# Row broadcasts and relayouts of an attention and MLP kernel by way of DRAM scratch

## Chip, cores, metric

One core of a Trainium2 chip. The time is device microseconds (us) of that core for one execution. The kernel is already tuned: before the change it takes 1255.33 us (median of 2 runs, 1255.06 to 1255.6). Engines in the profile: PE is TensorE's matrix multiply, PEld its weight load, DVE VectorE, ACT ScalarE, POOL GpSimd, SP SyncE, whose queue (SPq) issues every DMA that matters here. In the profile's lines `arena` is the kernel's buffer in SBUF (on-chip memory of 128 partitions), `psum` the banks that matmuls write, and sums, recips, rstd and heads are the new scratch buffers in DRAM.

## The reference, cut to what matters

```python
B, S, D, H = 1, 2048, 640, 32            # head size Dh = 20
xn = layernorm(x)
# A: attention
q, k, v = split(xn @ wqkv)               # 32 heads
p = softmax(q @ k.T * Dh**-0.5)          # 2048 x 2048 for each head
s = (p @ v) @ wo
# B: an MLP over columns and rows
h  = gelu(layernorm(xn) @ w1)
x1 = xn + shift4(h) @ w2                 # four column groups shifted by +1, -1, +2, -2 rows
g  = silu(x1 + gelu(layernorm(x1) @ w3) @ w4)
out = x + s * g
```

Softmax is the heavy part. ACT does most of the 134 million exponentials (860 instructions of 128x1024 in the profile), DVE the rest with integer arithmetic on the score's bits.

## The kernel before

The program is a list of tasks, each with an engine, an assumed duration, buffers read and written. A planner in the kernel's own source simulates the chip with these assumptions and so fixes the order of instructions on every engine. On the chip each engine runs its list in that order and stands still where the next instruction's input is not there: DVE stood still 203.0 us in all, 9.5 at most, before the 31 multiplies below, until a DMA had landed. What the planner assumes of DMA is these lines (nanoseconds; nbytes is what the author of the task passed in):

```python
SYNC_LAT = 130.0
self.dma_bw = 280.0
self.dma_lat0 = 1900.0
...
if t.is_dma and t.nbytes:
    xs = max(t.finish, dma_free)                    # transfers queue behind each other
    dma_free = xs + t.nbytes / self.dma_bw
    t.lat = dma_free + self.dma_lat0 - t.finish
...
si = min(range(len(ps)), key=lambda i: ps[i][0])    # PSUM bank: the one free first
```

Heads are taken in 8 quads of 4, each against 4 blocks of 512 query columns: 32 groups. After a group, four heads' results stand in one PSUM bank, 32 partitions apart, each with its row of sums at partition 32i+20. Dividing needs the reciprocals of that row on all partitions of the head:

```python
def normalise(...):                                  # cut
    T("dve", ..., tensor_copy(Ob, PV))                               # ob
    # z: four rows of sums, one partition each, to 32 partitions x 16
    T("sp", 240, [dma_start(ZT[32*i:32*i+32, ob, :], Ob[32*i+20:32*i+21, :]...) for i in range(4)], nbytes=16384)
    T("dve", ..., reciprocal(RZ, ZT))                                # rz
    # ra: back to one partition of each head
    T("sp", 240, [dma_start(RB[32*i:32*i+1, :]..., RZ[32*i:32*i+32, ob, :]) for i in range(4)], nbytes=8192)
    # rb: from that partition to 19 others
    T("sp", 240, [dma_start(RB[32*i+1:32*i+20, :], <RB[32*i] read 19 times>) for i in range(4)], nbytes=128*2048)
    T("dve", ..., tensor_tensor(On, Ob, RB, op=mult))                # on
    # od: four or five DMAs of 20 partitions at most into OTd
```

For the MLP's first layernorm, the row of 2048 values of 1/std has to be on every partition:

```python
T("sp", 60, dma_start(RR[0:1, :]..., T16[0:NT, :]), nbytes=8192, name="rr0")
T("sp", 60, dma_start(RR[1:128, :], <RR[0] read 127 times>), nbytes=1048576, name="rr1")
...
T("dve", ..., tensor_tensor(y2c, xnT, RR, op=mult))                  # y2
```

Here 60 is the assumed cost of one issue on SP's queue in nanoseconds, 240 that of four. Query and key weights come in eight DMAs of 20 columns per quad, into a buffer whose other columns are zero.

Of the kernel before, what the change touches and what calls it, by code (L numbers as in the profile page):

```python
# [90 lines left out]
class Task:  # L91
# [3 lines left out]
                 "acq", "rel", "stream", "sidx", "cls", "nbytes", "mode", "ndma", "tile")  # L95

    def __init__(self, tid, eng, dur, fn, reads, writes, due, name, lat, is_dma):
# [27 lines left out]
        self.tile = None  # L125


class Planner:
# [75 lines left out]
    def task(self, eng, dur, fn, reads=(), writes=(), due=None, name="", lat=0.0,  # L204
             is_dma=False, acq=None, rel=None, stream=None, after=(), cls=0, nbytes=0, mode=0, ndma=1, tile=None):
# [6 lines left out]
        t.tile = tile  # L212
        if is_dma and nbytes:
            t.lat = self.dma_lat0 + nbytes / self.dma_bw
# [55 lines left out]
    def schedule(self, verbose=False):  # L270
        tasks = self.tasks
        n = len(tasks)
# [43 lines left out]
        while done < n:  # L316
# [52 lines left out]
            if t.acq is not None:  # L369
                pname, handle = t.acq  # L370
                ps = pstate[pname]
                si = min(range(len(ps)), key=lambda i: ps[i][0])
                ft, rel_tid = ps[si]
                handle.slot = si
                held[id(handle)] = (pname, si)
                ps[si] = (INF, None)
                if rel_tid is not None:
                    t.preds.add(rel_tid)
                    tasks[rel_tid].succs.append((t.id, True))
# [272 lines left out]

def c_pool(n, kind="ts"):
    return 150 + (1.1 if kind == "ts" else 2.4) * n


class Gen:
# [71 lines left out]
    def build(self, plan_only=False):  # L729
        nc, pl = self.nc, self.pl  # L730
        with contextlib.ExitStack() as es:
# [3 lines left out]
            pl.init_arena(ARENA)  # L735
            self.W0 = 5
# [47 lines left out]
    def setup_consts(self):  # L784
# [22 lines left out]
        zw = self.zw = self.alloc("zw", [32], BF16)  # L807
        T("pool", 200, lambda e: e.memset(zw[:, :], 0.0), writes=[A("zw")], name="zw")
# [3 lines left out]
    def alloc_persistent(self):  # L812
# [9 lines left out]
        self.Wp = self.alloc("Wp", [2, KC, 128], BF16)  # L822
        T("dve", 700, lambda e: e.memset(self.Wp[:, :, :, :], 0.0), writes=[A("Wp", qk) for qk in range(2)], name="wp0")
# [13 lines left out]
        T("pool", 600, lambda e: e.memset(self.RB[:, :], 0.0), writes=[A("RB")], name="rb0")  # L837
# [15 lines left out]
    def load_inputs(self):  # L853
# [4 lines left out]
        for n0 in range(0, cfg.NT, 2):  # L858
            n1 = n0 + 2
            T("sp", 60, lambda e, n0=n0, n1=n1: e.dma_start(X[:, n0:n1, :], xv[:, n0:n1, :]),  # L860
# [135 lines left out]
    def prep_weights(self, q):  # L996
# [4 lines left out]
        for qk in (1, 0):  # L1001
            c0 = qk * D + q * cfg.QW
            T("sp", 240, lambda e, qk=qk, c0=c0: [e.dma_start(self.Wp[:, qk, :, 32 * i:32 * i + DH], src[:, :, c0 + DH * i:c0 + DH * i + DH])
                                                 for i in range(4)],
              writes=[A("Wp", qk)], is_dma=True, nbytes=128 * cfg.KC * 64 * 8, name=f"ld_wp{q}_{qk}", stream=f"wp{qk}", ndma=4)

    def prep(self, q):
# [6 lines left out]
        KC, NQC = cfg.KC, cfg.NQC  # L1014
        KT, QT, Wp, xnT = self.KT, self.QT, self.Wp, self.xnT
        for qk, dst, tag in ((1, KT, "KT"), (0, QT, "QT")):
            for c in range(NQC):
                c0 = 512 * c
                at = [A(tag, b, c)] + ([A("QTa", b, c)] if qk == 0 else [])
                h, wa = self.mm_tile(f"{tag}{q}_{c}", KC, 512, lambda k, j, qk=qk: Wp[:, qk, k, 32 * j:32 * j + 32],  # L1020
                                     lambda k, j, c0=c0: xnT[:, k, c0:c0 + 512],
                                     lambda k, qk=qk, c=c: [A("Wp", qk)] + [A("xnT", k, c)], at)
                if qk == 1:
                    T("dve", c_dve(512), lambda e, h=h, c0=c0: e.tensor_scalar(KT[:, b, c0:c0 + 512], self.wbank(h)[:, 0:512],  # L1024
                                                                               self.eaug[:, 0:1], None, op0=ALU.add),
                      reads=[wa, A("eaug")], writes=at, name=f"kev{q}_{c}", rel=h)
                elif q == 0:
                    T("act", c_act(512) + 100, lambda e, h=h, c0=c0: e.activation(QT[:, b, c0:c0 + 512], self.wbank(h)[:, 0:512], AF.Copy),
                      reads=[wa], writes=at, name=f"qev{q}_{c}", rel=h)
                else:  # L1030
                    T("dve", c_dve(512), lambda e, h=h, c0=c0: e.tensor_copy(QT[:, b, c0:c0 + 512], self.wbank(h)[:, 0:512]),
                      reads=[wa], writes=at, name=f"qev{q}_{c}", rel=h)
# [21 lines left out]
        T("sp", 240, lambda e: [e.dma_start(QT[20:128:32, b, 512 * c:512 * c + 512], SH[32 * c:32 * c + 4, :]) for c in range(NQC)],  # L1054
# [3 lines left out]
    def v_load(self, hf):  # L1058
# [5 lines left out]
        self.T("sp", 60, lambda e: e.dma_start(Wv[:, :, :], src[:, :, c0:c0 + D // 2]), writes=[self.A(f"Wv{hf}")], is_dma=True,  # L1064
# [30 lines left out]
    def attn_quad(self, quad):  # L1095
# [9 lines left out]
        for qc in range(NQC):  # L1105
# [3 lines left out]
            if col:  # L1109
                T("sp", 240, lambda e, qc=qc, gb=gb: [e.dma_start(self.QM[32 * i:32 * i + 32, gb, i, :],  # L1110
# [96 lines left out]
    def score_dve(self, b, qc, kt, a, quad):  # L1207
# [6 lines left out]
        for jj in range(2):  # L1214
# [3 lines left out]
              acq=("W", h), mode=1)  # L1218
# [16 lines left out]
    def normalise(self, quad, qc):  # L1235
# [28 lines left out]
        def fz(e):  # L1264
            out = []
            for i in range(4):
                z = Ob[32 * i + 20:32 * i + 21, :].rearrange("o (a b) -> o a b", b=16)
                out.append(e.dma_start(ZT[32 * i:32 * i + 32, ob, :], z))  # L1268
            return out
        T("sp", 240, fz, reads=[A("Ob")], writes=[A("ZT", ob)], is_dma=True, nbytes=16384, name=f"z{quad}_{qc}", stream="z", ndma=4)  # L1270
        T("dve", c_dve(16, "recip"), lambda e: e.reciprocal(RZ[:, ob, :], ZT[:, ob, :]),  # L1271
          reads=[A("ZT", ob)], writes=[A("RZ", ob)], name=f"rz{quad}_{qc}")
        def fb(e):
            out = []
            for i in range(4):
                out.append(e.dma_start(RB[32 * i:32 * i + 1, :].rearrange("o (a b) -> o a b", b=16), RZ[32 * i:32 * i + 32, ob, :]))  # L1276
            return out
        T("sp", 240, fb, reads=[A("RZ", ob)], writes=[A("RB")], is_dma=True, nbytes=8192, name=f"ra{quad}_{qc}", stream="ra", ndma=4)
        def fc(e):
            out = []  # L1280
            for i in range(4):
                r = RB[32 * i:32 * i + 1, :]
                src = bass.AP(r.tensor, r.offset, [list(r.ap[0]), [0, 19], [1, 512]])
                out.append(e.dma_start(RB[32 * i + 1:32 * i + 20, :], src))  # L1284
            return out
        T("sp", 240, fc, reads=[A("RB")], writes=[A("RB")], is_dma=True, nbytes=128 * 2048, name=f"rb{quad}_{qc}", stream="rb", ndma=4)
# [5 lines left out]
        moves, ats = [], []  # L1292
        for i in range(4):
            r0, at = DH * (4 * quad + i), 32 * i
            while r0 < DH * (4 * quad + i + 1):
                st, p0 = divmod(r0, 128)
                L = min(128 - p0, DH * (4 * quad + i + 1) - r0)
                moves.append((at, st, p0, L))
                ats.append(A("OTd", st, qc))
                r0, at = r0 + L, at + L  # L1300
        def fd(e):
            return [e.dma_start(self.OTd[p0:p0 + L, st, 512 * qc:512 * qc + 512], self.On[at:at + L, ob, :]) for (at, st, p0, L) in moves]
        T("sp", 60 * len(moves), fd, reads=[A("On", ob)], writes=sorted(set(ats)), is_dma=True, nbytes=80 * 1024, name=f"od{quad}_{qc}",
          stream="od", ndma=len(moves))

    def load_wo(self):
# [10 lines left out]
        T("sp", 60, lambda e: e.dma_start(Wo[:, :, :], self.aps["A_wo"].rearrange("(kc p) n -> p kc n", p=128)),  # L1317
# [3 lines left out]
        T("sp", 240, lambda e: [e.dma_start(Wo7[32 * i:32 * i + DH, :], self.aps["A_wo"][r0 + DH * i:r0 + DH * i + DH, :]) for i in range(4)],  # L1321
# [19 lines left out]
    def finish_qc(self, qc):  # L1341
# [8 lines left out]
        for nl in range(4):  # L1350
            n = 4 * qc + nl
            sl = n % 2
            T("sp", 60, lambda e, sl=sl, n=n: e.dma_start(XR[:, sl, :], xs[:, n, :]),
# [23 lines left out]
            T("sp", 60, lambda e, sl=sl, n=n: e.dma_start(outv[:, n, :], OS[:, sl, :]),  # L1377
# [15 lines left out]
    def b_alloc1(self):  # L1393
# [14 lines left out]
          reads=[A("tv", 1), A("mh2")], writes=[A("R2")], name="r2")  # L1408
        RR = self.RR = self.alloc("RR", [S], FP32)
# [160 lines left out]
```

## Time and profile before

The lines of the profile themselves are quoted in the prediction below.

| path (before) | assumed by the planner | measured | shortfall | DVE waits in all |
|---|---|---|---|---|
| reciprocal to multiply (ra, rb), 31 groups | 0.24+1.93+0.24+2.84+0.39 = 5.6 us | 12.3 us, median | 6.7 us x 31 = 208 us | 203.0 us |
| 1/std to first product (rr0, rr1), once | 0.06+1.93+0.06+5.65+0.39 = 8.1 us | 42.5 us | 34.4 us | 34.1 us |

The issue cost was assumed at 60 ns each and is about 590 to 690 (median of the lines of z, ra and rb).

### The profile page before, as it was taken

How to read it: one execution, taken by the hardware profiler on the slowest of the kernel's cores; microseconds unless marked ns; L12 is line 12 of the kernel's file. 1: busy time of each engine (PE TensorE's matmuls, PEld its weight loads, DVE VectorE, ACT ScalarE, POOL GpSimd, SP SyncE). 2: the span in 40 equal slices, each digit the busy share in tenths (PEclk: the TensorE clock that was granted, in tenths of full speed). 3: DMA queues.
4: the chain of work that ended last, by engine and by line, in shares of the span. 5: the costliest groups of instructions: out<-in, count | busy, mean ns of one | idle time of the engine just before them, and what ended most of it. 6: DMA issues, size and time to landing. Idle time of an engine off the chain costs nothing.

```text
span 1255.6 us, 35173 instructions
## 1 busy us (share of the span) xinstructions
PE 989.7 (79%) x15986; PEld 403.3 (32%) x15986; DVE 703.4 (56%) x1143; ACT 900.6 (72%) x937; POOL 30.4 (2%) x61
## 2 busy tenths in 40 slices
PE   4944887878787897789977896878879799767786
PEld 2411332323222334244322442323323243222343
DVE  7713766656565466465744474544566446556425
ACT  6752977868678775478866987776588787667684
POOL 6000000000000001000000000000000000000000
PEclk9986988889888888899988898898898889888897
DMA  6100110001002100210111010110101100100122
GB/s 170 18 23 18 15 16 14 13 14 16 14 14 87 18 13 12 51 34 12 18 45 42 13 14 24 37 43 10 21 17 37 44 14 11 42 13 12 36 66 75
DMA packets 109629, 37.87 MB, mean 30 GB/s; under 512 B 89685, under 2 KB 106997, under 8 KB 109353
## 3 DMA queue, kind: packets, MB, share of 16 engines
q1 hardware_dynamic: 109480, 35.62, 12.2%
q8 instruction: 125, 2.05, 0.7%
q14 instruction: 24, 0.20, 0.1%
HBM read 20.09 MB, written 2.62 MB: 18 GB/s over the span
## 4 chain that ended last, share of the span: by engine, by line
PE 37%; DMA 27%; SPq 14%; DVE 12%; ACT 8%; issue 2%; ACTq 0%; DVEq 0%
DMA arena<-arena 26%; PE psum L722 13%; PE psum L1193 12%; ACT arena L1200 7%; SPq L1284 5%; PE psum L1175 4%; PE psum L1164 4%; SPq L1276 4%; SPq L1268 3%; DVE arena L1225 2%; PE psum L1153 2%; DVE arena L1138 2%; DVE arena L1287 1%; DMA arena<-in_B_w_dram 1%; DVE arena L882 1%
## 5 line engine op out<-in xcount | busy, mean ns | idle before, releaser
L1200 ACT ACTIVATE arena<-psum 128x1024 bf16<-128x1024 f32 x860 | 817.2, 1035 | 327.9 <-PE psum L1193 209.5
L722 PE MATMUL psum<-arena 128*32 128x320 bf16 (+1 forms) x6224 | 399.1, 356 | 75.1 <-DMA arena<-in_B_w_dram 16.3
L1193 PE MATMUL psum<-arena 128*32 128x512 bf16 x5344 | 441.7, 410 | 11.6 <-ACT arena L1200 9.1
L722 PEld LDWEIGHTS psum<-arena 128*32 128x32 bf16 x6224 | 166.1, 101 | 247.8 <-issue 54.9
L1175 PE MATMUL psum<-arena 32*128 32x512 bf16 x712 | 137.9, 410 | 99.1 <-DVE arena L1225 53.8
L1138 DVE TENSOR_SCALAR arena<-arena 128x2048 uint16<-128x2048 uint16 x328 | 208.5, 687 | 7.4 <-PE psum L1153 5.9
L1193 PEld LDWEIGHTS psum<-arena 128*32 128x32 bf16 x5344 | 122.3, 101 | 178.7 <-ACT arena L1200 108.8
L1164 PE MATMUL psum<-arena 128*22 128x512 bf16 x1720 | 172.7, 404 | 1.2 <-ACT arena L1200 1.2
L1225 DVE TENSOR_SCALAR arena<-psum 128x1024 uint16<-128x1024 f32 x114 | 138.6, 1216 | 43.4 <-PE psum L1175 42.3
L1153 PE MATMUL psum<-arena 128*22 128x512 bf16 x1312 | 119.6, 402 | 37.1 <-DVE arena L1138 36.8
L1287 DVE TENSOR_TENSOR arena<-arena 128x512 bf16<-128x512 f32 x31 | 21.5, 692 | 203.0 <-DMA arena<-arena 203.0
L1175 PEld LDWEIGHTS psum<-arena 32*128 32x128 bf16 x712 | 31.1, 92 | 222.2 <-DVE arena L1225 70.1
L1228 DVE TENSOR_SCALAR arena<-psum 128x512 uint16<-128x512 f32 x100 | 63.9, 680 | 20.1 <-PE psum L1175 19.6
L1164 PEld LDWEIGHTS psum<-arena 128*22 128x22 bf16 x1720 | 45.3, 95 | 66.8 <-issue 35.1
L1153 PEld LDWEIGHTS psum<-arena 128*22 128x22 bf16 x1312 | 34.4, 96 | 82.2 <-DVE arena L1138 47.2
L1508 DVE CAST arena<-psum 128x512 bf16<-128x512 f32 x48 | 32.9, 687 | 44.5 <-PE psum L722 44.4
L1521 DVE TENSOR_TENSOR arena<-psum,arena 128x320 bf16<-128x320 f32 x32 | 15.2, 488 | 42.6 <-PE psum L722 42.6
L1024 DVE TENSOR_SCALAR arena<-psum,arena 128x512 bf16<-128x512 f32 x32 | 23.8, 746 | 13.2 <-PE psum L722 13.2
L1271 DVE RECIPROCAL arena<-arena 128x16 f32<-128x16 f32 x31 | 7.8, 251 | 41.5 <-DMA arena<-arena 41.5
L1442 DVE TENSOR_TENSOR arena<-arena 128x2570 bf16<-128x2570 bf16 (+1 forms) x4 | 11.3, 2833 | 34.1 <-DMA arena<-arena 34.1
L1372 DVE SCALAR_TENSOR_TENSOR arena<-psum,arena 128x320 bf16<-128x320 f32 x32 | 15.1, 486 | 26.7 <-PE psum L722 26.7
L1467 DVE TENSOR_TENSOR arena<-psum,arena 128x320 bf16<-128x320 f32 x32 | 15.6, 487 | 17.5 <-PE psum L722 17.3
(83 smaller groups left out, 351.2 us busy)
## 6 DMA issues: line engine op xcount, KB each, us to landing
arena<-in_B_w_dram SPq DMA_DIRECT2D x48, 160.0 KB, 2.7
arena<-arena SPq DMA_DIRECT2D x124, 38.0 KB
arena<-arena SPq DMA_DIRECT2D x124, 32.0 KB, 1.8
arena<-arena SPq DMA_DIRECT2D x248, 2.0 KB, 1.7
arena<-in_A_x_dram SPq DMA_DIRECT2D x8, 320.0 KB, 5.9
arena<-in_A_x_dram SPq DMA_DIRECT2D x16, 160.0 KB, 2.4
out_dram<-arena SPq DMA_DIRECT2D x16, 160.0 KB, 2.0
arena<-arena SPq DMA_DIRECT2D x96, 20.0 KB
```

What stands on the lines that cost most here:

```text
L722: ins = e.matmul(pb[32 * c:32 * c + 32, 0:N], lhsT(k, c), rhs(k, c), start=(k == 0), stop=(k == nk - 1), tile_position=(0, 32 * c))
L1138: lambda e, s=s, v=v: e.tensor_scalar(SS[:, s, :], U[:, :], 0.5, EXP_B[v], op0=ALU.mult, op1=ALU.add),
L1153: ins = e.matmul(pb[32 * i:32 * i + 22, 0:512], w, SS[:, s, at:at + 512].bitcast(BF16), start=False, stop=final, tile_position=(0, 32 * i))
L1164: ins = e.matmul(pb[32 * i:32 * i + 22, 0:512], VA[:, ql, kts[i // 2], i, :], PT[:, slots[i // 2], 512 * (i % 2):512 * (i % 2) + 512], sta ...
L1175: return e.matmul(out, self.KT[32 * i:32 * i + 32, b, 128 * kt:128 * kt + 128], self.QT[32 * i:32 * i + 32, b, 512 * qc:512 * qc + 512], s ...
L1193: ins = e.matmul(self.bank(2 * sb + jj)[32 * c:32 * c + 32, :], self.KT[:, b, 128 * kt + 32 * c:128 * kt + 32 * c + 32], self.QM[:, gb, 2 ...
L1200: lambda e: e.activation(self.PT[:, slot, :], self.psum[:, 1024 * sb:1024 * sb + 1024], AF.Exp, scale=cfg.scale),
L1225: return e.tensor_scalar(dst, self.psum[:, 512 * (self.W0 + lo):512 * (self.W0 + hi + 1)], a_exp, EXP_BIAS, op0=ALU.mult, op1=ALU.add)
L1228: ins = e.tensor_scalar(dst[:, 512 * k:512 * k + 512], self.bank(self.W0 + s)[:, :], a_exp, EXP_BIAS, op0=ALU.mult, op1=ALU.add)
L1268: out.append(e.dma_start(ZT[32 * i:32 * i + 32, ob, :], z))
L1276: out.append(e.dma_start(RB[32 * i:32 * i + 1, :].rearrange("o (a b) -> o a b", b=16), RZ[32 * i:32 * i + 32, ob, :]))
L1284: out.append(e.dma_start(RB[32 * i + 1:32 * i + 20, :], src))
```

## The change

Six things are changed together. (1) The row of 1/std goes to DRAM and comes back to all 128 partitions in one DMA. (2) The chain of a group does the same: sums to DRAM, back as 128x16, reciprocals to DRAM, back as 128x512, one issue each. (3) A group's result goes to DRAM and back for the change of layout. (4) A quad's weights are loaded as 92 dense columns; the columns that belong to a neighbouring head are zeroed by a mask in the PSUM evacuation. (5) The planner picks PSUM banks so that two tiles that DVE could evacuate together lie side by side. (6) The planner assumes 660 ns for each DMA issue on SP in place of 60. The intent is a shorter chain: few DMAs, over many engines (the old row of 1/std ran at a DMA share of 0.06, a sixteenth).

```diff
# cut to its core; every other T("sp", 60, ...) also becomes T("sp", C_SP, ...)
+C_SP = 660
# (5) planner
-                si = min(range(len(ps)), key=lambda i: ps[i][0])
+                idle = [i for i in range(len(ps)) if ps[i][0] <= st + 1e-9]
+                if idle:
+                    ...                 # beside its partner, else at the edge or the middle
+                else:
+                    si = min(range(len(ps)), key=lambda i: ps[i][0])
# (2) chain; z and r0 (one DMA each) and back
-        T("sp", 240, fz, ..., name=f"z{quad}_{qc}", ndma=4)
+        T("sp", C_SP, lambda e: e.dma_start(dz[ob], Ob[20:128:32, :]), ..., nbytes=8192, name=f"z0{quad}_{qc}")
+        T("sp", C_SP, lambda e: e.dma_start(ZT[:, ob, :], dz[ob].rearrange("i (a b) -> (i a) b", b=16)), ..., nbytes=8192, name=f"z1{quad}_{qc}")
...
-        T("sp", 240, fb, ..., name=f"ra{quad}_{qc}", ndma=4)
-        T("sp", 240, fc, ..., name=f"rb{quad}_{qc}", ndma=4)
+        T("sp", C_SP, lambda e: e.dma_start(dr[ob].rearrange("i (a b) -> (i a) b", b=16), RZ[:, ob, :]), ..., nbytes=8192, name=f"r0{quad}_{qc}")
+        T("sp", C_SP, lambda e: e.dma_start(RB[:, :], bass.AP(dr.tensor, dr[ob].offset, [[512, 4], [0, 32], [1, 512]])), ...,
+          nbytes=128 * 2048, name=f"r1{quad}_{qc}")
# (3) heads
+        T("sp", C_SP, lambda e: e.dma_start(do[ob], self.On[:, ob, :]), ..., name=f"o0{quad}_{qc}")
+        ...                             # o1: do -> OTd, 1 to 4 DMAs
# (1) row of 1/std
-        T("sp", 60, lambda e: e.dma_start(RR[0:1, :]..., T16[0:NT, :]), name="rr0")
-        T("sp", 60, lambda e: e.dma_start(RR[1:128, :], bass.AP(RR.tensor, RR.offset, [list(RR[0:1, :].ap[0]), [0, 127], [1, S]])), name="rr1")
+        T("sp", C_SP, lambda e: e.dma_start(dq.rearrange("(n p) -> n p", p=128), T16[0:NT, :]), name="rr0")
+        T("sp", C_SP, lambda e: e.dma_start(RR[:, :], bass.AP(dq.tensor, dq.offset, [[0, 128], [1, S]])), name="rr1")
# (4) weights and mask
-            T("sp", 240, ... [e.dma_start(self.Wp[:, qk, :, 32*i:32*i+DH], src[:, :, c0+DH*i:c0+DH*i+DH]) for i in range(4)], ndma=4)
+            T("sp", C_SP, ... e.dma_start(self.Wp[:, qk, :, :], src[:, :, c0:c0 + 92]))
...
-    e.tensor_scalar(KT[...], psum, self.eaug[:, 0:1], None, op0=ALU.add)
+    e.tensor_scalar(KT[...], psum, mask[:, 0:1], self.eaug[:, 0:1], op0=ALU.mult, op1=ALU.add)
```

## The prediction

> **What bounds the kernel now.** I read the page's busy shares first, then the waits, then the timeline of one group, then busy time by stretch. There are 32 groups of attention (8 quads of heads, 4 column blocks each); after each but the last the 128x512 result must be divided by row sums which are carried to all partitions by DMA.
>
> ```profile
> PE 989.7 (79%) x15986; PEld 403.3 (32%) x15986; DVE 703.4 (56%) x1143; ACT 900.6 (72%) x937; POOL 30.4 (2%) x61
> PE 37%; DMA 27%; SPq 14%; DVE 12%; ACT 8%; issue 2%; ACTq 0%; DVEq 0%
> DMA arena<-arena 26%; PE psum L722 13%; PE psum L1193 12%; ACT arena L1200 7%; SPq L1284 5%; PE psum L1175 4%; PE psum L1164 4%; SPq L1276 4%; SPq L1268 3%; DVE arena L1225 2%; PE psum L1153 2%; DVE arena L1138 2%; DVE arena L1287 1%; DMA arena<-in_B_w_dram 1%; DVE arena L882 1%
> ```
>
> No engine is full, and 41% of the chain of work that ended last is DMA and its queue (the second line; the third is 26% for copies within SBUF alone). Who waits is in the view of waits (waiter, line, releaser: us in total, times, longest):
>
> ```profile
> ACT arena L1200 <- PE psum L1193: 209.5, 103, 34.5
> DVE arena L1287 <- DMA arena<-arena: 203.0, 31, 9.5
> DVE arena L1271 <- DMA arena<-arena: 41.5, 25, 4.8
> DVE arena L1442 <- DMA arena<-arena: 34.1, 1, 34.1
> ```
>
> L1287 is the multiply by the reciprocals, once per group: DVE stands still 203.0 us for it. L1271 is the reciprocal, L1442 the first product with the row of 1/std. ACT's exp (L1200) is the one that suffers, through PE. How, the timelines of DVE, PE and DMA queue show (start, us, ..., idle before and releaser in brackets):
>
> ```profile
> 512.20 0.69 DVE L1287 TENSOR_TENSOR arena<-arena 128x512 bf16<-128x512 f32 x1 [8.61 <-DMA arena<-arena]
> 512.81 1.22 DVE L1225 TENSOR_SCALAR arena<-psum 128x1024 uint16<-128x1024 f32 x1
> 514.08 1.47 PE L722 MATMUL psum<-arena 128*32 128x512 bf16 x12 [8.64 <-DVE arena L1225]
> 545.17 2.42 SPq L1268 DMA_DIRECT2D arena<-arena  x4
> 550.13 2.44 SPq L1276 DMA_DIRECT2D arena<-arena  x4
> 553.74 3.46 SPq L1284 DMA_DIRECT2D arena<-arena  x4
> ```
>
> DVE runs in a fixed order, so while L1287 waits it drains no PSUM; three working banks fill, PE stops (8.64 us), ACT runs dry. The last three lines are another group's chain: sums out (from 545.17), reciprocals in (550.13), rows spread (553.74, done when L1287 starts at 561.82). Busy time by stretch (window, length, PE, PEld, DVE, ACT, POOL, PE clock, DMA share, GB/s):
>
> ```profile
> 80.00:110.00 30.00, 0.00 (x0) 0.00 (x0) 1.26 (x1) 0.00 (x0) 0.00 (x0) 0.55 0.06 25
> 505.50:512.20 6.70, 0.00 (x0) 0.00 (x0) 0.00 (x1) 1.50 (x2) 0.00 (x0) 0.81 0.17 47
> 514.00:520.80 6.80, 6.28 (x68) 2.23 (x72) 3.72 (x7) 2.56 (x3) 0.00 (x0) 0.57 0.28 63
> 233.00:257.00 24.00, 23.67 (x418) 9.66 (x410) 16.23 (x27) 23.83 (x26) 0.00 (x0) 1.00 0.04 10
> sum 652.80, PE 615.50 PEld 253.63 DVE 453.22 ACT 590.66 POOL 4.26; mean PE 21.22 PEld 8.75 DVE 15.63 ACT 20.37 POOL 0.15
> ```
>
> First: for 30 us all engines stand still for the row of 1/std, with a DMA share of 0.06, one engine of sixteen. Second and third: a stall, then PE busy but at clock 0.57. Fourth: between stalls PE and ACT are both full. Last: the sum of 29 stretches, each from 8 us after one stall to the start of the next; there PE is 94% and ACT 90% busy.
>
> [...]127 rows of 8 KB in 40.7 us at share 0.06. [...]1.04 MB / 40.7 us = 25.6 GB/s. [...]Here a 2 KB SBUF copy lands in 1.7 us and a 160 KB store to DRAM in 2.0, so DRAM looks little dearer. [...]eight L1193 matmuls take 1.07 us after a stall, 0.61 otherwise.
>
> **The change part by part.**
> (1) Row of 1/std. Now 127 rows from one partition, one engine, 40.7 us. New: 8 KB to DRAM, then 128 rows[...]; with the write before it (2.0 against 1.7) about 7 us for what took 42.5. ACT's gap of 34.5 us goes but for 0 to 3: minus 33.
> (2) Chain of one group. Now, median over the 31 groups, 12.3 us from end of reciprocal to start of multiply, and about 4 from the copy of PSUM to the reciprocal. The pieces: 4 issues 2.4 us, 1.75 from last issue to landing, again 2.4 and 1.75, then 4 issues 3.46 and 5.73 to landing[...]. New, one issue each: sums to DRAM 2.0, back 2.1, reciprocal 0.25, to DRAM 2.1, broadcast. [...]So 4.1 up to the reciprocal (no gain) and 6.5 after it: estimate 10.8 against 16.5, 5.8 saved.
> (3) What DVE has to do meanwhile. In the built order I multiplied the instructions between the three by their mean times in the profile: before, 3.7 us ahead of the reciprocal and 5.4 between it and the multiply, on average; after, 6.0 and 5.7, because the planner now counts 660 ns per issue and four trips. Against 4.1 and 6.5, and with DVE 69% busy at the undisturbed pace (5.7 of work lasts about 8), most waits should vanish. A few groups have only 1 to 3.5 us of work in the second gap (worst 1.0, 1.4, 1.9, 3.3). Estimated rest: 15 to 40 us of DVE wait in all instead of 244.
> (4) Small things. Weights: 2 issues of 92 columns per quad in place of 8 of 20, off the path. Masking rides on evacuations that exist: 28 copies of 686 ns become multiplies from PSUM (like L1228's kind, 680 for the same size), 4 on ACT get a scale. Bank choice: 100 evacuations of 680 ns become 4, and 114 of 1216 become 162: 48 x (1360 - 1216) = 7 us of DVE, not its bound. Head transposes by way of DRAM have no reader until the end. PE and ACT keep every instruction of theirs.
>
> The sum, two ways. (a) From ACT's timeline: its idle inside the 31 DVE waits plus the 5 us after each is 191 us, of which 9% (15 us) is the ordinary pace of those 5 us: 176. With 33: minus 209, giving 1046. (b) From pace: from 115 to 1230 us ACT has 827 us of work; at 0.905 busy that takes 914. PE has 912 busy, of which 174 at half clock; at full clock (0.61/1.07) about 837, at 0.943 it takes 888. The slower, 914, replaces 1115: minus 201; with 33, minus 234, giving 1021. The middle, 1034, plus about 8 for remaining waits: 1040.
>
> **The rivals.** First, the wait moves: four dependent trips through DRAM could take 2.5 to 3 us each rather than 2 (the smallest loads of weights took 2.5), making 6.5 into 8 after the reciprocal. [...]Against: DVE has 5.7 us of work there. It would leave 2 us a group, some 60 us of DVE wait[...]: about 1085. Second, PE becomes the bound and gives the gain back: it needs 913 us at full clock in the whole kernel[...]. Against: in dense stretches the clock is 1.00, and the halves follow idleness. With the clock at 0.94 throughout: about 1090. Third, the DVE waits are hidden anyway, and only the 1/std row pays: 1220. Against: ACT is idle through and after most of them. Fourth, the SP queue, in order, waits between dependent trips, and holds weight loads for the MLP behind it (PE now waits 16.3 us for those): plus 10 to 30.
>
> **Range and chances.** Predicted 1040 us. 1000 would need a pace better than between stalls today; 1095 holds the first or second rival. Faster by over 2%: 0.97; within 2%: 0.02 (it would need the stalls and the row both to persist); slower: 0.01.
>
> **What would show each step.** (1) right if DVE's wait before the y product is under 4 us and all engines run through 80 to 110 us. (2) right if the stretch from reciprocal to multiply, where DVE does wait, is 6 to 7 us, with the broadcast 4 to 4.5 from issue to landing. (3) right if the DVE wait at the multiply falls from 203 to under 40 and the PE clock's mean rises from 0.89 to above 0.95. The pace is right if ACT between 115 us and the end's last 25 is about 90% busy. I am wrong if the DVE waits go and ACT stays below 85% busy, which would mean another bound I did not see, or if the multiply still waits over 3 us a group.

The forecast came to 1040 us: sum (a) 1046, sum (b) 1021, their middle 1034, plus about 8 for remaining waits. Some terms of the sum: in (1) the copy to 128 rows, 4.6 us of the "about 7"; in (2) the new broadcast, 4.3 us of the 6.5 after the reciprocal. 4.6 and 4.3 were estimates; nothing had shown them then. "One engine" is read off a DMA share of 0.06, a sixteenth.

## The result, and the profile after

After: 975.93 us median (974.78 and 977.09) against 1255.33; ratio 0.7774, interval 0.7734 to 0.7814. A ratio here is the mean time of one kernel's fast runs over that of the other's in the same rounds, so not quite the ratio of the medians quoted. All runs were fast, except one of before (1264.88 us, in the rounds of e7, e10, e11 and e12), which the ratios leave out; all gave correct results. The prediction was 1040 with a range from 1000 to 1095: the direction was right, the time is 24 us under the range.

The page after: busy shares, then the chain of work that ended last by engine.

```profile
PE 905.6 (93%) x15986; PEld 382.8 (39%) x15986; DVE 706.0 (73%) x1096; ACT 888.6 (91%) x937; POOL 29.7 (3%) x59
PE 49%; ACT 39%; DVE 6%; DMA 4%; issue 1%; SPq 0%; POOL 0%; DVEq 0%
```

PE was at 79% and is at 93%, with the same 15986 instructions; its busy time fell by 84 us at a higher clock (0.888 and 0.993, below), and the mean of 5344 score matmuls (L1193, after L1213) from 410 to 381 ns. DMA and its queue held 41% of the chain that ended last and hold 4%. PE and ACT now share it, 49 and 39%. The row of granted PE clock over 40 slices (tenths), before and after:

```profile
PEclk9986988889888888899988898898898889888897
```

```profile
PEclk9999999999999999999999999999999999999998
```

The mean went from 0.888 to 0.993. A slice of before is 31 us, about one group long, and so held a stall and the low clock after it (0.57 in 514 to 520.8 us) nearly every time.

The waits of the kernel after (waiter, line, releaser: us in total, times, longest). L1295 is the multiply, L1289 the reciprocal, L1220 ACT's exp:

```profile
DVE arena L1295 <- DMA arena<-recips: 15.7, 14, 2.3
DVE arena L1289 <- DMA arena<-sums: 1.0, 2, 0.7
ACT arena L1220 <- PE psum L1184: 42.2, 21, 9.1
```

The multiply waited 203.0 us and waits 15.7; the reciprocal 41.5 and now 1.0. ACT's largest wait for PE was 209.5 us and is 42.2. No line is left in which DVE waits for the row of 1/std: the product with it ran at 63.40 us, straight behind other work, in the timeline. The same view has one group's chain (start, us, engine, line; idle before in brackets), near the same time as the one that the prediction shows:

```profile
63.40 2.83 DVE L1460 TENSOR_TENSOR arena<-arena 128x2570 bf16<-128x2570 bf16 x1
...
515.46 0.25 DVE L1289 RECIPROCAL arena<-arena 128x16 f32<-128x16 f32 x1
515.74 0.34 SPq L1291 DMA_DIRECT2D recips<-arena  x1
517.97 0.58 SPq L1293 DMA_DIRECT2D arena<-recips  x1
523.30 0.69 DVE L1295 TENSOR_TENSOR arena<-arena 128x512 bf16<-128x512 f32 x1 [1.97 <-DMA arena<-recips]
```

From the end of the reciprocal (515.71) to the multiply (523.30) are 7.6 us, and here DVE did wait, so this is the chain's own length: 2.2 to the second issue, then 0.58 of issue and 4.75 to landing. Over all groups the median is 7.8 us where it was 12.3. What single transfers take is in the list of DMAs (size of each, median us to landing):

```profile
arena<-rstd SPq DMA_DIRECT2D x1, 1024.0 KB, 4.7
arena<-sums SPq DMA_DIRECT2D x31, 8.0 KB, 1.7
recips<-arena SPq DMA_DIRECT2D x31, 8.0 KB, 1.4
```

The row of 1/std, 40.7 us before, lands in 4.7, and small trips to and from DRAM take 1.4 to 1.7 in the median.

Busy time by stretch (window, length, PE, PEld, DVE, ACT, POOL, PE clock, DMA share, GB/s). First the main stretch of before, then three of after, which together hold the same work and the tail:

```profile
115.00:1230.00 1115.00, 912.48 (x14510) 366.50 (x14506) 632.60 (x987) 826.68 (x839) 7.13 (x15) 0.89 0.11 26
```

```profile
78.00:115.00 37.00, 34.49 (x594) 13.33 (x590) 27.93 (x37) 36.94 (x39) 0.00 (x0) 1.00 0.09 25
115.00:945.00 830.00, 794.47 (x13876) 330.99 (x13868) 606.59 (x902) 781.64 (x806) 7.07 (x15) 1.00 0.16 42
945.00:973.00 28.00, 18.59 (x420) 10.35 (x420) 16.92 (x37) 12.76 (x14) 0.00 (x0) 0.88 0.27 84
```

The counts nearly match: 839 ACT instructions before, 844 after (39+806, one of them counted on both sides of 115). Work that began at 115 now begins at about 78, or at 82.9 if one goes by the same ACT instruction, the 87th; so the row of 1/std and what went with it gave back 32 to 37 us. From 78 to 945 are 867 us in place of 1115; ACT is busy 818.6 of them (36.94+781.64), 94.4%. That percentage is where the prediction went wrong.

### The profile page after: what moved, and what is told of

It is laid out like the page before. It is cut to its first block, busy times and chain, and to the rows that moved or that the text cites. A ratio compares the mean times of both kernels' runs of the same rounds, so it can differ in the third digit from the quotient of the medians.

```text
span 973.1 us, 34801 instructions
## 1 busy us (share of the span) xinstructions
PE 905.6 (93%) x15986; PEld 382.8 (39%) x15986; DVE 706.0 (73%) x1096; ACT 888.6 (91%) x937; POOL 29.7 (3%) x59
## 3 DMA queue, kind: packets, MB, share of 16 engines
q1 hardware_dynamic: 80132, 43.09, 15.9%
## 4 chain that ended last, share of the span: by engine, by line
PE 49%; ACT 39%; DVE 6%; DMA 4%; issue 1%; SPq 0%; POOL 0%; DVEq 0%
ACT arena L1220 36%; PE psum L738 19%; PE psum L1213 17%; PE psum L1184 5%; PE psum L1195 4%; PE psum L1173 3%; DMA arena<-recips 3%; DVE arena L1245 1%; ACT arena L1530 1%; DVE arena L1158 1%; DMA arena<-in_B_w_dram 1%; DVE arena L901 1%; ACT arena L1543 1%; DVE arena L1460 1%; DVE arena L1043 1%
## 5 line engine op out<-in xcount | busy, mean ns | idle before, releaser
L1220 ACT ACTIVATE arena<-psum 128x1024 bf16<-128x1024 f32 x860 | 805.1, 1039 | 56.9 <-PE psum L1184 42.2
L1213 PE MATMUL psum<-arena 128*32 128x512 bf16 x5344 | 408.2, 381 | 14.9 <-ACT arena L1220 12.3
L738 PE MATMUL psum<-arena 128*32 128x320 bf16 (+1 forms) x6224 | 366.2, 336 | 14.9 <-DVE arena L1043 6.5
L1245 DVE TENSOR_SCALAR arena<-psum 128x1024 uint16<-128x1024 f32 x162 | 197.5, 1219 | 62.0 <-PE psum L1195 60.8
L738 PEld LDWEIGHTS psum<-arena 128*32 128x32 bf16 x6224 | 161.2, 97 | 161.0 <-issue 23.5
L1213 PEld LDWEIGHTS psum<-arena 128*32 128x32 bf16 x5344 | 107.9, 95 | 172.3 <-ACT arena L1220 136.4
L1184 PE MATMUL psum<-arena 128*22 128x512 bf16 x1720 | 163.3, 381 | 0.1
L1195 PE MATMUL psum<-arena 32*128 32x512 bf16 x712 | 125.3, 385 | 11.8 <-ACT arena L1220 6.4
L1173 PE MATMUL psum<-arena 128*22 128x512 bf16 x1312 | 112.9, 380 | 1.9 <-DVE arena L1158 1.7
L1526 DVE CAST arena<-psum 128x512 bf16<-128x512 f32 x48 | 33.1, 689 | 42.6 <-PE psum L738 42.6
L1539 DVE TENSOR_TENSOR arena<-psum,arena 128x320 bf16<-128x320 f32 x32 | 15.7, 491 | 38.4 <-PE psum L738 38.2
L1295 DVE TENSOR_TENSOR arena<-arena 128x512 bf16<-128x512 f32 x31 | 21.3, 687 | 15.8 <-DMA arena<-recips 15.7
L1043 DVE TENSOR_SCALAR arena<-psum,arena 128x512 bf16<-128x512 f32 x32 | 25.5, 803 | 4.5 <-PE psum L738 4.4
L1474 DVE CAST arena<-psum 128x512 bf16<-128x512 f32 x20 | 13.8, 689 | 18.0 <-PE psum L738 18.0
L1282 DVE COPY arena<-psum 128x512 f32<-128x512 f32 x31 | 21.3, 688 | 6.2 <-PE psum L1184 5.9
L1050 DVE TENSOR_SCALAR arena<-psum,arena 128x512 bf16<-128x512 f32 x28 | 20.8, 747 | 5.9 <-PE psum L738 5.7
```

The costliest lines, as they stand in the source:

```text
L738: ins = e.matmul(pb[32 * c:32 * c + 32, 0:N], lhsT(k, c), rhs(k, c), start=(k == 0), stop=(k == nk - 1), tile_position=(0, 32 * c))
L1043: T("dve", c_dve(512), lambda e, h=h, c0=c0: e.tensor_scalar(KT[:, b, c0:c0 + 512], self.wbank(h)[:, 0:512], mask[:, 0:1], self.eaug[:, 0: ...
L1173: ins = e.matmul(pb[32 * i:32 * i + 22, 0:512], w, SS[:, s, at:at + 512].bitcast(BF16), start=False, stop=final, tile_position=(0, 32 * i))
L1184: ins = e.matmul(pb[32 * i:32 * i + 22, 0:512], VA[:, ql, kts[i // 2], i, :], PT[:, slots[i // 2], 512 * (i % 2):512 * (i % 2) + 512], sta ...
L1195: return e.matmul(out, self.KT[32 * i:32 * i + 32, b, 128 * kt:128 * kt + 128], self.QT[32 * i:32 * i + 32, b, 512 * qc:512 * qc + 512], s ...
L1213: ins = e.matmul(self.bank(2 * sb + jj)[32 * c:32 * c + 32, :], self.KT[:, b, 128 * kt + 32 * c:128 * kt + 32 * c + 32], self.QM[:, gb, 2 ...
```

## The experiments

Four questions were asked: which of the six parts pays; which of the planner's costs; whether the route by DRAM pays as such or only because the planner's assumption comes true with it; and what limits a row broadcast. My theory at first was that the DRAM route shortens the chain and so removes the waits. The rivals: the planner's issue cost (6) orders the work better, whatever the route; bank choice (5) saves DVE work; and, later, the planner's ignorance of DMA times is the whole trouble. Letters in the expectations are names for such theories. The kernels ran on four chips, on which before took 1250 to 1259 us in the median; the ratios allow for that, the medians do not. Where a difference is small both are given; a difference of 0.001 in the ratio is 1.3 us. The summary:

| run | built from | median us (range) | ratio to before, interval |
|---|---|---|---|
| after | | 975.93 (974.78-977.09) | 0.7774, 0.7734-0.7814 |
| e1_nobank | after, old bank choice | 976.41 (974.49-979.7) | 0.7756, 0.7718-0.7795 |
| e2_oldcost | after, issue cost 60 | 1003.69 (998.48-1008.02) | 0.7982, 0.7934-0.803 |
| e3_routes_only | after, both planner changes undone | 1008.67 (1004.91-1011.3) | 0.8008, 0.7968-0.8047 |
| e4_bank_only | before, new bank choice | 1256.52 (1252.79-1266.65) | 0.9991, 0.993-1.0052 |
| e10_chaincost | after, 660 for the chain only | 988.68 (987.01-992.5) | 0.7897, 0.7849-0.7945 |
| e11_othercost | after, 660 for all but the chain | 984.57 (982.65-984.92) | 0.7856, 0.7821-0.7891 |
| e12_longchain | after, 1300 for the chain | 974.52 (974.01-976.31) | 0.7781, 0.7746-0.7816 |
| e17_w3cost | e10 and MLP weight loads | 985.21 (983.0-991.19) | 0.784, 0.7786-0.7894 |
| e18_qmcost | e10 and query copies | 983.6 (982.13-987.2) | 0.7824, 0.7765-0.7883 |
| e6_bank_cost | before, (5) and (6) | 1047.77 (1046.58-1049.82) | 0.8373, 0.8336-0.8409 |
| e7_honest | e6, planner told true landings | 988.14 (986.24-989.49) | 0.7886, 0.785-0.7922 |
| e14_honest_rr | e7, 1/std by DRAM | 978.02 (977.84-979.86) | 0.7817, 0.7784-0.785 |
| e8_oldrr | after, old 1/std row | 1018.07 (1016.32-1022.93) | 0.814, 0.81-0.8179 |
| e9_sbrr | after, 1/std from one partition to 128 | 1010.76 (1008.27-1013.94) | 0.8084, 0.8041-0.8126 |
| e16_tree | after, 1/std within SBUF in two steps | 983.03 (982.25-984.35) | 0.7816, 0.7769-0.7863 |
| e20_spread | e16, middle rows four apart | 978.18 (975.75-979.84) | 0.777, 0.7714-0.7826 |
| e13_r1x4 | after, spread as four DMAs | 973.99 (972.55-976.29) | 0.7745, 0.7698-0.7792 |

### Which part pays

e1_nobank undoes the bank choice in the kernel after. It tells whether part (5) is worth the few us of DVE that the prediction gave it.

```diff
-                idle = [i for i in range(len(ps)) if ps[i][0] <= st + 1e-9]
-                ...
+                si = min(range(len(ps)), key=lambda i: ps[i][0])
```

> The changed kernel with the old choice of PSUM bank (lowest free time) put back, all else changed. Theory E (the pace between the old stalls was still slowed by them; the DMA routes alone bring the gain): 975 to 990 us, DVE waits at the multiply still under 30 us. Rival B (the pace came from pairs of score tiles in neighbouring banks, which spare DVE's split evacuations and PE's waits for banks): 1005 to 1030 us, with about 100 evacuations of 680 ns back and PE waiting over 40 us for them.

976.41, the same as after. The bank choice is worth nothing that can be measured here.

e2_oldcost undoes only the planner's issue cost.

```diff
-C_SP = 660
+C_SP = 60
```

> The changed kernel with the planner told 60 ns per DMA issue as before, all else changed. Theory E: 975 to 995 us; the planned chain becomes some 2.4 us shorter than real, so DVE waits at the multiply grow from 16 to 40-70 us but stay under 3 us each[...]. Rival C (the pace came from the planner's true issue cost, which orders all engines better): 1010 to 1040 us.

1003.69, 28 us slower than after (26 by the ratios), which lies between the two ranges. With 60 assumed, DVE waits 31.3 us at the multiply and 8.7 at the reciprocal, against 15.7 and 1.0. Nothing that moves data differs from the kernel after; only the order does. So a number in the planner is worth 28 us.

e3_routes_only undoes both (the two edits above), which leaves the routes by DRAM and the dense weights.

> The changed kernel with both planner changes undone: DMA routes, dense weights and mask alone. Theory E: 980 to 1005 us. B and C together: 1035 to 1060 us, near the forecast of 1040.

1008.67: parts (1) to (4) alone take 247 of the 279 us; this too lies between the two ranges, 4 us over the first. The intervals of e2 and e3 overlap, so the bank choice is not seen here either.

e4_bank_only puts the bank choice into the kernel before, in the same lines as the change has it.

> The kernel before with the new bank choice alone. Theory E: 1245 to 1256 us (7 us of DVE work less, stalls unchanged at 203 us). Rival B: 1215 to 1235 us.

0.9991: nothing. Theory E's upper end was 1256, the run took 1256.52.

### Which of the planner's costs

e10_chaincost assumes 660 ns for the four DMAs of the chain alone (z0, z1, r0, r1) and 60 for all others; e11_othercost the reverse. If the gain of part (6) came from DVE's wait at the multiply, e10 should have it in full.

```diff
-C_SP = 660
+C_SP = 60
+C_CH = 660
-        T("sp", C_SP, lambda e: e.dma_start(dz[ob], ...
+        T("sp", C_CH, lambda e: e.dma_start(dz[ob], ...      # also z1, r0, r1; e11: C_SP = 660, C_CH = 60
```

> The changed kernel, planner told 660 ns only for the four DMAs of the normalise chain and 60 ns for all other DMAs. Told 60 ns for all, it took 1004 us; told 660 for all, 976. Theory D (what the true cost buys is distance: DVE's multiply is placed later, and each us of DVE wait saved is a us of time): 976 to 985 us, DVE wait at the multiply 15 to 20 us. Rival S (it buys a better order of the in-order DMA queue and of all else): 995 to 1005 us.

> The complement: 60 ns for the chain's four DMAs, 660 ns for all others. Theory D: 995 to 1005 us, DVE wait at reciprocal and multiply about 40 us together. Rival S: 976 to 985 us.

988.68 and 984.57. Each half gives part of it; e10 is in neither range, e11 in that of rival S. e11, whose DVE waits at the multiply are 32.0 us, twice those of e10 (14.4), is if anything the faster (4 us in the same rounds, the runs' ranges apart). So DVE's wait is not what these us go by. One thing that the other issues do change is in the view of waits: PE's wait for the streamed MLP weights, before, after and in e10 (one line of each).

```profile
PE psum L722 <- DMA arena<-in_B_w_dram: 16.3, 8, 4.0
```

```profile
PE psum L738 <- DMA arena<-in_B_w_dram: 0.3, 1, 0.3
```

In e10 this wait is 6.2 us. That is a part of the 12.7 us between e10 and after at most.

e17_w3cost and e18_qmcost add one kind of issue to e10 each, to find the one that matters: the loads of MLP weights, or the copies of queries.

```diff
-T("sp", C_SP, lambda e, ws=ws, fc=fc: e.dma_start(W3s...          # e17; C_SP is 60
+T("sp", 660, lambda e, ws=ws, fc=fc: e.dma_start(W3s...
-T("sp", 4 * C_SP, lambda e, qc=qc, gb=gb: [e.dma_start(self.QM... # e18
+T("sp", 2640, lambda e, qc=qc, gb=gb: [e.dma_start(self.QM...
```

> Planner told 660 ns for the chain and for the 48 loads of MLP weights, 60 ns for the rest (with the chain alone it was 988.7, with all 976). Theory W (PE's 6 us of waits for these weights and what follows from them make the difference): 975 to 980 us, PE's wait for them under 1 us. Otherwise 985 to 990.

> Planner told 660 ns per issue for the chain and for the 124 query copies (2.6 us a group), 60 ns for the rest. If these make the difference: 975 to 980 us. Otherwise 985 to 990.

985.21 and 983.6: neither gives the 12.7 us alone (3.5 and 5 by the medians, 7 and 9 of 15 by the ratios), and their ranges overlap. PE's wait for weights is 4.0 and 1.8 us. Which issue costs improve the order, and how, stays open.

e12_longchain tells the planner that the chain is longer still (C_CH = 1300, others 660), so that it puts more work between reciprocal and multiply. If what is left of DVE's waits still costs time, this should gain; the theory that it does expected 958 to 968.

> The changed kernel, planner told 1300 ns for each of the chain's four DMAs, 660 for the others: 2.6 us more distance per group. Theory D: the 16.7 us of DVE waits fall under 4 us and the time to 958 to 968 us. Rival: DVE's multiply is no longer what limits, 973 to 980 us.

```profile
DVE arena L1296 <- DMA arena<-recips: 3.9, 5, 1.3
```

The multiply waits 3.9 us in all in place of 15.7, and the time is 974.52, the same. So the waits of after, 2.3 us at most, cost nothing that can be measured. The theory fell.

### The route, or the plan?

e6_bank_cost is the kernel before with the planner's two changes and none of the routes: every 60 becomes 660, every 240 becomes 2640.

```diff
-        T("sp", 240, fc, ..., name=f"rb{quad}_{qc}", ndma=4)
+        T("sp", 2640, fc, ..., name=f"rb{quad}_{qc}", ndma=4)     # and so for all; bank choice as in (5)
```

> The kernel before with both planner changes (bank choice, 660 ns per issue) and all its old DMAs and their assumed landing times. The twelve issues of a group's chain now count 7.2 us more. Theory P (the planner's ignorance was the cost): DVE waits at the multiply fall from 203 to 20-60 us, the gap of the 1/std row stays at some 30 us, time 1025 to 1060. Rival R (the routes by themselves): over 1150 us.

1047.77: 208 of the 279 us, with every DMA still the old one. Its waits:

```profile
DVE arena L1300 <- DMA arena<-arena: 50.6, 25, 4.4
DVE arena L1455 <- DMA arena<-arena: 35.2, 1, 35.2
```

The multiply's wait (L1300) fell from 203.0 to 50.6 us. The row of 1/std (L1455) keeps its wait in full, for its time was mistaken in the assumed bytes per ns and not in the issue.

e7_honest goes on from e6 and corrects these two as well. It passes the planner sizes that make the assumed landings true (3.57 + 1.9 = 5.5 us for rb, 38.2 + 1.9 = 40.1 for rr1). The DMAs themselves are still those of before. If the chain's length is what costs, this stays near e6; if it is the order, it comes near to after.

```diff
-  ... nbytes=128 * 2048, name=f"rb{quad}_{qc}"
+  ... nbytes=1000000, name=f"rb{quad}_{qc}"
-  ... nbytes=1048576, name="rr1"
+  ... nbytes=10700000, name="rr1"
```

> The kernel before with its old one-partition DMAs, but new bank choice, 660 ns per issue, and the planner told the landing times measured (about 5.5 us for the spread, 40 us for the row of 1/std). Theory P (what cost the time was that the planner did not know the DMAs were slow; slow but known they can be hidden): 985 to 1030 us, DVE wait at the multiply under 60 us. Rival R (the slow routes cost by themselves[...]): 1080 to 1200 us.

988.14, which is 267 of the 279 us and faster than the routes alone (e3). One group in its timeline (L1284 reciprocal, L1289 the four ra, L1297 the four rb, L1300 multiply):

```profile
528.44 0.25 DVE L1284 RECIPROCAL arena<-arena 128x16 f32<-128x16 f32 x1
543.18 0.69 DVE L1300 TENSOR_TENSOR arena<-arena 128x512 bf16<-128x512 f32 x1 [0.78 <-DMA arena<-arena]
```

```profile
529.26 2.44 SPq L1289 DMA_DIRECT2D arena<-arena  x4
534.64 3.45 SPq L1297 DMA_DIRECT2D arena<-arena  x4
```

From reciprocal to multiply are 14.5 us, longer than in before (the median is 13.9 against 12.3), yet DVE waited 0.78 us: the planner gave it other work for the rest. In the whole run DVE waits 4.5 us at the multiply and 6.9 at the reciprocal:

```profile
DVE arena L1284 <- DMA arena<-arena: 6.9, 7, 2.8
DVE arena L1300 <- DMA arena<-arena: 4.5, 6, 1.1
```

So the chain's length as such cost nothing measurable here, where there was other work to put in; what cost was an order made for a chain half as long. What e7 still lacks to after shows as one gap of 15.9 us in ACT at 122 us, when the first gelu waits for what comes of the late 1/std row.

e14_honest_rr therefore takes e7 and moves only the row of 1/std to DRAM, the two lines of part (1).

> The kernel that told the planner the true times of the old DMAs (988 us), with the row of 1/std by way of DRAM in addition; the normalise chain, head copies and weights stay the old one-partition DMAs. If the DRAM route of the chain is worth nothing once the planner knows the times: 970 to 980 us, as the changed kernel. If it is worth something: 983 to 990.

978.02, ratio 0.7817 (0.7784 to 0.785) against 0.7774 (0.7734 to 0.7814) of after: not clearly apart. With the planner told the truth, the new routes of chain, heads and weights together are worth 2 us by the medians and 5 by the ratios; up to some 12 are not excluded. The median from reciprocal to multiply is 13.8 us in this kernel and 7.8 in after.

### What limits a row broadcast

e8_oldrr puts the old row of 1/std back into the kernel after (127 rows from one partition; the planner still thinks it takes some 9 us).

```diff
-  e.dma_start(RR[:, :], bass.AP(dq.tensor, dq.offset, [[0, 128], [1, S]]))
+  e.dma_start(RR[1:128, :], bass.AP(RR.tensor, RR.offset, [list(RR[0:1, :].ap[0]), [0, 127], [1, S]]))
```

> The changed kernel with the row of 1/std spread by the old way (one partition to 127, one DMA engine), planner ignorant of it as before. If its price is the gap it makes: 33 us as forecast, 1005 to 1012 us. If one stall also slows what follows: over 1015. If the planner's other changes hide it: under 990.

1018.07: the row costs 42 us (1018.07 - 975.93; 46 by the ratios), not the 33 of the prediction. DVE's wait is 35.5 us and ACT's gap 34.1. The PE clock is at 0.50 in the stall and stays there for some 5 us after PE starts again (106.6 to 111.6 us), but that is not the difference: of ACT's instructions, counted in order in the profiled runs, the 81st starts 35 us later than in after, the 121st 37 and the last 48. The rest comes bit by bit over the whole run, and why is open. e9, next, has the same gap (34.3) and costs 35 us (39 by the ratios).

e9_sbrr asks for the reason of the 40 us. The prediction took the number of DMA engines at work for the limit (a share of 0.06, one engine's worth of sixteen); that is theory K, and X that a source of one partition is slow whatever the share. So this copies from a single partition of another buffer to 128 rows, in SBUF, without DRAM: a DMA share of 0.94, as it turned out, from one source partition as before.

```diff
+  RS = alloc("RS", [S], FP32)                                    # rr0 writes RS[0:1]
-  e.dma_start(RR[:, :], bass.AP(dq.tensor, dq.offset, [[0, 128], [1, S]]))
+  e.dma_start(RR[:, :], bass.AP(RS.tensor, RS.offset, [list(RS[0:1, :].ap[0]), [0, 128], [1, S]]))
```

> The changed kernel with the row of 1/std spread from one SBUF partition again, without DRAM, but to 128 partitions from a row outside the destination. Theory K[...]: lands in 4 to 7 us, 974 to 979 us. Rival X (one partition as source is slow whatever the engines, as the change's title has it): 20 to 40 us to landing, 990 to 1010 us.

1010.76, and the landing takes 40.0 us. Five us of the transfer in e9, then the same in e8 (columns as above; the last three are PE clock, DMA share, GB/s):

```profile
75.00:80.00 5.00, 0.00 (x0) 0.00 (x0) 0.00 (x0) 0.00 (x0) 0.00 (x0) 0.50 0.94 26
```

```profile
75.00:80.00 5.00, 0.00 (x0) 0.00 (x0) 0.00 (x0) 0.00 (x0) 0.00 (x0) 0.50 0.06 26
```

The DMA share goes from 0.06 to 0.94, from one engine's worth to nearly that of all sixteen, and the rate stays at 26 GB/s. So the number of engines was not the limit, and my reason in the prediction was wrong; that its time came out (4.6 us estimated for the new copy, 4.7 measured) was luck, for one source partition gives 26 GB/s here, and a sixteenth of the 418 GB/s that the row's way from DRAM shows in after (below) is 26 too. What e8 and e9 have in common is the single source partition.

e16_tree and e20_spread test this. Both go within SBUF by way of 16 rows. e16 puts them on neighbouring partitions, 0 to 15; e20 on 0, 4, ..., 60. The expectation of e16 counted 26 GB/s for each source partition and gave the second step 2.5 us; e20, with the rows apart, was set up when e16 had been run.

```diff
# cut; the planner is told 131072 * 12 bytes for the first step
+  e.dma_start(RS[0:16, :],    <row read 16 times>)               # e16; e20: RS[0:64:4, :]
+  e.dma_start(RR[:, :],       <RS[0:16] read 8 times each>)      # e20: RS[0:64:4]
```

> The changed kernel with the row of 1/std spread within SBUF in two steps: one partition to 16 (128 KB), then 16 partitions to 128 (1 MB). Theory X (one SBUF partition gives about 26 GB/s, whatever the engines): first step 5 us of data, second 2.5, some 11 us with the fixed parts, DVE's wait at the product under 8 us, time 976 to 986. Rival (copies within SBUF of rows this wide are slow anyhow): the second step takes over 15 us, time over 990.

> The two-step spread within SBUF of the run before it, with the 16 middle rows on partitions 0, 4, ..., 60 in place of 0 to 15. If neighbouring partitions share one path of some 26 GB/s[...]: the second step lands in 5.5 to 8 us against 12.1, DVE's wait at the product falls from 7.5 us to under 3, and the time from 983 to 975-979. If each partition or the copy within SBUF limits: 12 us again, 983.

The two steps of e16 in its list of DMAs (size of each, us to landing), then the second step of e20:

```profile
arena<-arena SPq DMA_DIRECT2D x1, 1024.0 KB, 12.1
arena<-arena SPq DMA_DIRECT2D x1, 128.0 KB, 6.6
```

```profile
arena<-arena SPq DMA_DIRECT2D x1, 1024.0 KB, 7.1
```

The second step lands in 12.1 us from 16 neighbours, which refutes the count by partitions, and in 7.1 in e20 from 16 partitions four apart; taking off the 1.7 us that a 2 KB copy needs in before, 1.05 MB move, as an estimate, at 101 and 194 GB/s, about four and seven and a half times the 26 of one partition. The first step, 128 KB out of one partition, again comes to 27 GB/s (0.131 MB in 6.6-1.7 us). The second step in e16 and in e20, and a us of the same row's way from DRAM in after:

```profile
60.00:70.00 10.00, 7.53 (x81) 2.03 (x80) 2.73 (x3) 9.61 (x11) 0.00 (x0) 0.98 0.94 98
```

```profile
60.00:65.00 5.00, 4.81 (x61) 1.37 (x60) 2.73 (x3) 5.00 (x7) 0.00 (x0) 1.00 0.93 197
```

```profile
61.00:62.00 1.00, 1.00 (x14) 0.21 (x12) 0.97 (x2) 1.00 (x2) 0.00 (x0) 1.00 0.99 418
```

The DMA share is 0.94, 0.93 and 0.99, the rate 98, 197 and 418 GB/s: the engines are as busy as in e9, and within SBUF the rate went by where the source lies: 26 GB/s from one partition (e9), 98 from 0 to 15, 197 from 0, 4, ..., 60. Why neighbours gave half of what the rows four apart gave, no run shows. In time e16 is 983.03 and e20 978.18; by the ratios neither is clearly apart from after. From DRAM the row lands in 4.7 us. The old spread of reciprocals (rb) read four single partitions at a DMA share of 0.06 to 0.07 (557 to 560 us in before), one engine's worth; no run separates the two there.

e13_r1x4 takes the spread of reciprocals, whose source has 4 as its slowest dimension, apart into four DMAs of 32 rows (and four issues, which the planner is told), to see whether the one copy is held to the four engines' worth of its DMA share in after (0.26 to 0.27 in 83 to 85 us).

```diff
-  e.dma_start(RB[:, :], bass.AP(dr.tensor, dr[ob].offset, [[512, 4], [0, 32], [1, 512]]))
+  [e.dma_start(RB[32*i:32*i+32, :], bass.AP(dr.tensor, dr[ob].offset + 512*i, [[0, 32], [1, 512]])) for i in range(4)]
```

> The changed kernel with the spread of reciprocals from DRAM as four copies of 32 rows each (slowest dimension 32 on both sides) in place of one whose source has 4 as its slowest. If the one copy runs on 4 engines, as forecast: the last of the four lands under 4.5 us after the first issue although three more issues (1.8 us) go ahead, against 5.0 to 5.3; time within 5 us of 976 because DVE waits there only 16 us in all. If the one copy already used 16: it lands later than now, 5.5 us or more.

Each copy lands in 2.0 us instead of about 5 and the last of the four 3.4 us after the first issue in the median, so here, with DRAM as the source, the form of the one copy did limit it; that the number of engines is the reason fits its share in after, but the share in e13 was not read. No multiply waits, and the time is 973.99: not clearly better than after, as e12 would lead one to expect. This and e12 (974.52) are the lowest times, and neither is distinguishable from 975.93. No version beats the change.

## Why the prediction was right, and where it was wrong

**The step that failed** is sum (b), "From pace": "from 115 to 1230 us ACT has 827 us of work; at 0.905 busy that takes 914." Measured, the same work holds ACT busy for 818.6 us and takes 867, a pace of 0.944. Of the 47 us, 9 come from less ACT time (818.6 / 0.905 would still be 905), the other 38 from the pace. Then the 8 us added for remaining waits, and the averaging with sum (a) at 1046, pushed the time up by 19 more. With 78 us for the start and a tail of 28 the span adds up: 78 + 867 + 28 = 973.

**Why the pace was mis-sized.** I measured 0.905 in the stretches of before that I called undisturbed, and took it for a property of the work. It goes with the order that the planner makes. e3 has the new routes and the planner of before; this is its stretch from the 87th to the 924th ACT instruction (columns as above):

```profile
80.50:981.00 900.50, 843.91 (x14530) 351.11 (x14522) 637.38 (x993) 817.27 (x840) 7.07 (x15) 0.98 0.15 40
```

ACT is busy 0.908 of it, nearly the pace forecast, and the whole time of e3, 1008.67, lies in the range forecast. Between the same two instructions it is 0.916 in e2 and 0.944 (862.6 us) after, and e2 and after differ in nothing but the assumed issue cost. The prediction named part (6) only for the instructions it puts between reciprocal and multiply, and gave it no worth of its own; e2 shows 28 us. What the better order consists in was not settled (e10, e11, e17, e18).

The stretches were not undisturbed either. Each runs from 8 us after one multiply to the start of the next multiply's wait, and so through the wait at the reciprocal, 41.5 us in all in before and 1.0 in after. Worked out from the traces again (30 stretches), ACT's share in them is 0.904 in before and 0.943 after, which is some 25 us over the 660 us that they last in before; 12 of these 25 lie between the start of the wait at the reciprocal and that at the multiply. An echo of the multiply's own stall is not the whole of it: starting 14 us after the multiply, the shares are 0.907 and 0.930.

**Sum (a)** counted ACT's idle in DVE's waits and the 5 us after them, and so could not see a loss of order spread over all the rest.

**Step (1), the row of 1/std.** DVE's wait went, as predicted, and engines run through 80 to 110 us. The size predicted was 33; measured are 32 to 37 at the start of the work, 35 in e9 and 42 in e8, whose further loss is unexplained. The reason given, one engine of sixteen, fell with e9: at a DMA share of 0.94 the copy was as slow (40.0 us). That it is where the source lies rests on e16 and e20 (98 and 197 GB/s).

**Step (2), the chain.** 6.5 us after the reciprocal were predicted. In the trace the reciprocals have landed 6.1 to 8.7 us after it, 7.1 in the median. The broadcast was sized too small, 4.3 predicted and 4.6 to 5.3 from issue to landing, the write to DRAM ahead of it too large, 2.1 and 1.4, and the two cancel: where nothing held it up, the chain took 6.1 to 6.5. The missing term is the time to the second issue. In the 14 groups where DVE waited that came 2.4 us after the first in the median in place of 1.4, because the write landed late or SP's queue issued another DMA first, and the chain was 7.9 us. The forecast put the broadcast on four engines, and the trace agrees: windows of a single us in it show a DMA share of 0.24 to 0.27 where it is alone, four engines' worth of sixteen. No gain up to the reciprocal was predicted and none came (median 4.6 before, 6.3 after). The pieces that the prediction lists for the old chain sum to 13.3 us after the reciprocal, not 12.3: 5.73 counts from the start of the last issue, which 3.46 already holds, and so does 1.75.

**Step (3), the waits.** Predicted 15 to 40 us in place of 244; measured 16.7. Clock above 0.95 predicted; 0.993 measured. But why they went is only half as predicted. The shorter chain is one way to it. e7 has the longer chain and fewer waits still. What removes a wait is that the planner's figure and the chip's agree: before 5.6 (0.24+1.93+0.24+2.84+0.39) assumed against 12.3, after 6.5 (0.66+1.93+0.66+2.84+0.39) against 7.8, in e7 13.1 (2.64+1.93+2.64+5.47+0.39) against 13.9. As a measure of the wait, shortfall (measured less assumed) times uses holds for before (6.7 us x 31 = 208 against 203.0; for the row of 1/std, once, 42.5 less 8.1 (0.06+1.93+0.06+5.65+0.39) = 34.4 against 34.1) but overstates smaller ones: after, 1.3 x 31 = 40 us against 15.7.

**Step (4), small things,** off the path: nothing speaks against it. The bank choice is worth nothing (e1, e4); weights and heads were not undone alone, but e14 has both in the old form and is not clearly slower.

**The rivals.** Waits moved into the new trips: no, 16.7 us in all. PE as the bound by a falling clock: no, the clock is 0.993, though PE is now 93% busy. Everything hidden but the row: no. The SP queue: it did hold the chain's second issue in some groups, within the 16.7 us; the wait for MLP weights, which I had feared for, fell from 16.3 to 0.3 us.

**The expected gain, split two ways.** Routes first: 247 us from parts (1) to (4), then 33 from the planner's numbers. Plan first: 208 from the issue cost, 60 more from true landings, 10 from the row of 1/std by DRAM, and 2 (5 by the ratios), not distinguishable from nothing, from all other routes. Both are true. The two remedies cover the same loss, and only for the row of 1/std is a worth of its own shown when the plan is right.

## What to carry to other kernels

Where a planner fixes the order of engines, compare its assumed time of each DMA path with the trace before changing the path: the shortfall times the number of uses (6.7 us x 31) was the wait in before, and correcting the assumed times (with the bank choice, worth nothing) brought 267 of 279 us. A pace read between stalls belongs to that order, and to whatever other stalls lie in the stretch, so do not carry it over to a kernel that is ordered anew. Broadcast a row from DRAM (here 4.7 us) or from source partitions that lie apart (7.1 us from 16 of them four apart, 12.1 from 16 neighbours, 40.0 from one), and do not judge a transfer by the busy share of the DMA engines: at 0.94 and at 0.06 it moved the same 26 GB/s.
